# A dilated convolution with gate and projection: thirteen against sixteen six-row groups, and every instruction's place written out

## The chip, the core and the metric

One core of a Trainium2 chip. TensorE does the matrix products into PSUM, VectorE and ScalarE read PSUM and SBUF, GpSimd reads and writes SBUF only, SyncE (SP) issues loads and stores, and 16 DMA engines move the data. The metric is the device time of one execution in microseconds (us): the median of several runs, lower is better.

## What is computed

```python
B, T, D, K = (2, 16000, 256, 3)            # x [B,T,D], w [K,D,2D], w_o [D,D], all bf16
def reference(x, w, w_o):
    dil = 2; pad = (K - 1) * dil
    xp = jnp.pad(x, ((0, 0), (pad, 0), (0, 0)))
    h = jnp.einsum('btc,cd->btd', xp[:, pad:pad + T, :], w[0])
    for i in range(1, K):
        off = pad - i * dil
        h = h + jnp.einsum('btc,cd->btd', xp[:, off:off + T, :], w[i])
    f = h[..., :D]; g = h[..., D:]
    z = jnp.tanh(f) * _sigmoid(g)
    return z @ w_o
```

So h[t] = x[t] w[0] + x[t-2] w[1] + x[t-4] w[2], then a gate, then a projection.

## The kernel before

**Groups.** Time steps are cut into groups. A group has R columns (256 as a rule) and J rows a column: J consecutive time steps. It is computed in four blocks, one for each 128 of the 512 channels of h (two for tanh, two for sigmoid). A block's *product* is two matmuls of 128x128 weights with 2R columns each. There are three kinds of group:

- P, the first 160 columns of the first sequence (J=4): the taps are multiplied directly (`direct`), while weights and inputs are still on their way.
- B (J=4): a fast form of the convolution with four products a block in place of six: m and p with the weights (w0+w2 -+ w1)/2, d0 with w2, d3 with w0. The inputs m, p, d0, d3 are sums or differences of the transposed x (the tile `xt`).
- A (J=6): five products a block for six rows: "first" (u1, with combined weights `wa_sb`), "mid" (rm), "last" (rp), "zero" (r0), "inf" (ri). The inputs u0, u1, u2, e, f are sums of `xt`; u3, uh, ud are u1 times 1/3, -1/2, 2; and rm = e+u3, rp = f+u1, r0 = u0+uh, ri = u2+ud are made on top of e, f, u0, u2.

Sequence one has 6 A, sequence two 7 A, the rest is B: ten with R=256, one with 160, one with 128.

**A block's steps**, as letters of the plan. TensorE: F (first), M (mid, A only), L (last), Z (zero), I (inf); each adds to the PSUM bank b, except I, which adds to the bank a. ScalarE: c copies bank b after F to SBUF (`ss`). VectorE: h makes hh = 1.5 ss - b after M (A only); a makes the bank a = 3 ss + b (A) or -2 ss + b (B) after L, and I is added on top; y makes yy = 2 hh + b (A only). ScalarE then applies tanh or sigmoid to b after Z (letter b), to yy (letter y) and to a after I (letter a). VectorE's g multiplies the tanh and sigmoid parts (`zz`, `zo`). TensorE's P projects a piece of 256 rows with four matmuls of 256 columns, into `o_ps`; e (ScalarE) or v (VectorE) evicts it to `osb`, and SP stores a finished `osb`.

**Who makes the inputs.** VectorE makes u0, u1, u2, e, f, u3, uh, ud, and m, p, d0, d3 of some B groups; GpSimd makes the other B inputs and ri, in quarters of 256 columns. rm, rp, r0 are accumulating DMAs issued from GpSimd's queue (`BY_DMA`). The helper `hold` makes each of GpSimd's sums wait for a VectorE instruction: the one noted last (`made_v[-1]`) or, with n primes on the token, n further back, so that it runs beside a VectorE instruction that reads PSUM.

**The order.** `seq` is the order of the blocks: four B groups, then A and B blocks mixed evenly, then the last B group. `PLAN` has one line for each place k of `seq`; its four columns are the orders of TensorE, ScalarE, VectorE and GpSimd in that place, where block k has its F, block k-1 its L and a, and so on. Loads (transposing DMAs on SP) are issued up to `LOAD = 15` blocks before they are wanted; there are four `xt` buffers for each J. Each engine and each queue runs its own instructions in the order in which they are issued.

Of the kernel before, what the change touches and what calls it, by code (L numbers as in the profile page):

```python
# [11 lines left out]

PLAN = """
 |  | m.0 d3.0 p.0 d0.0 G | 
F D D | c w |  | 
F L D | c d | a d3.1 G | wa.4 wa.3
F L Z I P P | c b e | a | wa.6
Z L F I | a b c | m.1 d0.1 p.1 a | wa.12'
F L Z I | a c b | m.2 g a | wa.5
L P F Z I | a e c b | d3.2 a | wa.2'  # L20
Z L F I | a b c | d0.2 u0.0 g a | wa.7
F L Z I | a c b | f.0 u1.0 a | wa.1
L F Z I | a c b | p.2 a u2.0 g | wa.14'
L Z F I P | a b e c | e.0 d3.3 a | wa.0
F P P Z L I | a c e e b | p.3 ud.0 g a | wa.11
L F I Z P P | a c b | u1.1 m.3 m.4 a | rp.0 ri.0'
F L Z P I P | a e e e b c | u3.0 e.1 uh.0 a d0.3 f.2 g | wa.10
F I Z L P | a c e b | u1.2 a | rm.0 ri.0'
L F Z I | a e c b | a g | r0.0
L Z I F P | a b c | u3.1 p.4 a | wa.8  # L30
Z L F P I | a b c e e | u0.1 uh.2 f.1 a d0.4 g | ri.0'
F I L P Z M P | c e a b | d3.4 u2.1 ud.1 a h | rp.1 rm.1 wa.15' wa.13' wa.9'
F Z L M I | a c e e b | g uh.1 a y h | d3.5' d3.5' ri.0'
P P Z F L I | y a b c | u3.2 e.2 a y | r0.1 ri.1 m.5
F L I Z M | a c y b | a u0.2 h | d0.5 d0.5
Z F L I M | a b c e | g a y h | r0.2 d0.5 ri.1
F P Z I L | a e c b y | g u2.2 a y | rm.2 ri.1 m.5' d0.5
F L P I Z M | a e c y b | a e.3 h | p.5
Z F I L M | a c b | g a y h | p.5 p.5 ri.1
P P F Z L I | a e e y c b | u0.3 a y | m.5 m.5'  # L40
L F I Z M | a c y b | ud.2 a u1.3 h | ri.2 ri.2'
Z P P F L I P M | a b e c e e | g u3.3 a y h | rp.2 p.5' p.6' d0.6'
F Z I L P | a e b c y | f.3 g a y | ri.2 d3.5
F L I Z M | a c y b | a u2.3 h | d3.5
Z F I L M P P | a c b e | g a y h | rp.3 rm.3 d0.6 ri.2
F Z I L P | a e e y b c | uh.3 e.4 ud.3 a y | d3.6 p.6 ri.3''
F L I Z M | a c y b | a u1.4 h | ri.3
Z F I L M P P P | a c b e | g a y h | m.6 d3.6
F Z P L I | a e y c b e e e | g u0.4 u3.4 f.4 a y | r0.3 ri.3 m.6''
F L P I Z M | a c y b | a ud.4 h | d0.6 d3.6 m.6  # L50
Z I F L | a b c | g a y | ri.3 m.6
F L P I Z M P | c a y b | u2.4 a h | ri.4' d3.6
F Z L I P M | a e e c b | e.5 uh.4 y a h | rp.4 p.6
F Z P L I | a y c b e e | g f.5 a y | rm.4 p.6' d0.6'
F P L Z M I | a c y b | g a h | r0.4 p.7 p.7 ri.4 d3.7 d3.7 m.7
F Z L P M I | a c e b e | u1.5 a y h | ri.4
I Z P L F P P | a e e b c y | u0.5 a y | ri.4
F L Z I M | a c b y | ud.5 u1.6 u2.5 a h u3.5 g | rp.5 ri.5''
F P Z L I P M | a c e e b | a y h | rm.5 d0.7 p.7
F Z I L P | a e y b c e | g uh.5 a y | m.7' ri.5  # L60
F L I Z P M | a c y b | g ud.6 a h | r0.5 ri.5' m.7'
F P Z L M I | a c b e e | e.6 uh.6 y a h | d3.7 d0.7
F P Z L I P | y e a b c | f.6 a y | m.7' ri.5
F L Z M I P | a c y b e | u0.6 g h u3.6 a | rp.6 p.7' d0.7' d0.7
F L P M Z I | a c e e e b | y a h | rm.6
Z I L F P | a y b c | u2.6 u1.7 a y g | m.8' m.8'
F P P L Z M I | a c e y b e e | g u3.7 a h | r0.6 ri.6' d3.7'
F Z L P I M | a c b | e.7 ud.7 a y h | p.8' ri.6' ri.6
F Z I L P P | a y b c | u0.7 u2.7 a y | p.8' ri.6'
F L P M Z I | a e c y e e b | uh.7 f.7 a h g | d0.8' ri.7'  # L70
Z I F L | a b c | u1.8 a y | rm.7 rp.7 m.8'
F P P L Z M I | a c e y b e | g a e.8 h | d3.8 ri.7
F Z I L M P | a c b e | g a y ud.8 h | p.8 d3.8 ri.7
F P Z I L P | a e c y b e | u3.8 f.8 a y | r0.7 d3.8' d0.8
L F I Z M P | a e c b y | a u0.8 h | d0.8 m.8
F Z P L P M I P | a c e e e b | e.9 g a y h | p.8 ri.7
Z F L I | a b c y | u1.9 g a y | rp.8 d3.8
F L I Z M P P | a c e b y | u2.8 ud.9 a h | rm.8 d0.8 d3.9'
Z F L P M P I P | a e c e e b | uh.8 g a y h | ri.8 ri.8
Z L F I | y a b e c | u3.9 u2.9 a y | r0.8 ri.8  # L80
F I Z L M P P | a c y b | f.9 u0.9 a h | ri.9' ri.8'
F L Z I M | a e e c b | g y a h | ri.9
F Z I L | y a b c e | f.10 g a y | rp.9 d0.9
F P P L Z M I | c a b y | u0.10 a h | rm.9 d0.9'
F Z I L P P M | a e c e b | e.10 g uh.9 y a h | r0.9 d3.9
F P Z L P I | a e e y b c e | m.9 u1.10 a y | ri.9' ri.9
F L I Z M P | c a e b y | p.9 a h | d0.9' d3.9' d3.9'
Z P F L I M | a b c e e | ud.10 g a y h | d0.9
F I Z P L P | a y b c | u2.10 g a y | rp.10 ri.10 d3.10 d0.10
F L I Z M | a c e y b | a u1.11 h |   # L90
Z P F L P I | a b c e | u3.10 g y uh.10 a | rm.10 ri.10'
F L P Z I M | a e c b e y | e.11 a u2.11 h | ri.10'
F I Z L P P M | c a e b | ud.11 f.11 a y u3.11 h | r0.10 ri.10'
F I Z L | a e c y b e | g uh.11 a y | d3.10 d0.10'
L P F P Z M I | a c b y | g a h | rm.11 d0.10 d3.10
F Z L I M P | a c e b | u1.12 a y h | ri.11' ri.11'
F Z I L | a e c b y | p.10 m.10 y a | rp.11 ri.11
L P F P Z M I | a c e b y e | a u3.12 u0.11 h f.12 g | d3.10
Z F P L I P M P | a c b e | a y h | r0.11 ri.11 d0.10
I F Z L P | a e y e b e c | g e.12 ud.12 y a | rm.12  # L100
F P P M Z L P I | c e a b y e | p.11 u2.12 uh.12 a h g | d3.11' ri.12'
F I L P Z M P | a c e b | y a h | d0.11 d3.11
F Z L P I | y e a b c e e | u0.12 m.11 a y | rp.12 r0.12 ri.12''
F P Z L M I | c a b y | a h g | 
F Z L P I M P | a c b e e e | a y h | d0.11 ri.12
F Z L P I | a c b e y | g a y | d3.11 ri.12
L F I Z M P | a c y b e e | a g h | 
Z F L P I P M | b c a | y a h | 
F P Z L I | a e e y b c e | y a | d0.11
F P L Z M I | c a b y | a h g | d0.11  # L110
F P L Z I P | a e c b e | a y | d3.11
F I Z L | a c y b | g a | 
L P I F Z P | a e b c e | a g | 
Z I F L P P | a c b E | a v | 
L Z I P p | a b | a g v | 
Z I P p P | a e b | v | 
H H | a e E | g v | 
R R |  |  | 
 | e | v | 
# [4 lines left out]
def kernel(  # L124
# [7 lines left out]

    nc = tc.nc
# [15 lines left out]
    LOAD = 15  # L151
# [4 lines left out]
    LEAD, TRAIL = 4, 0  # L156
    N_A = (6, 7)
    groups, of_kind = [], {"P": [], "A": [], "B": []}

    def group(kind, b, t, R):  # L160
        of_kind[kind].append(len(groups))
        groups.append(dict(kind=kind, b=b, t0=t, R=R, J=ROWS[kind]))
        return t + ROWS[kind] * R

    for b in range(B):
        t = 0
        if b == 0:
            t = group("P", b, 0, 160)
        rows = (T - t - 6 * RG * N_A[b]) // 4
        n_a, n_b = N_A[b], rows // RG - (0 < rows % RG < P)  # L170
        for n in range(max(n_a, n_b)):
            if n < n_b:
                t = group("B", b, t, RG)
            if n < n_a:
                t = group("A", b, t, RG)
        rows = (T - t) // 4
        while rows:
            t = group("B", b, t, 160 if rows % P else P)
            rows = (T - t) // 4
    As, Bs = of_kind["A"], of_kind["B"]  # L180
    mixed = [[(g, oi) for g in gs for oi in range(4)] for gs in (As, Bs[LEAD:-1 - TRAIL])]
    seq = [(g, oi) for g in Bs[:LEAD] for oi in range(4)]
    took = [0, 0]
    while took != [len(m) for m in mixed]:
        nxt = 0 if took[0] * len(mixed[1]) < took[1] * len(mixed[0]) else 1
        seq.append(mixed[nxt][took[nxt]])
        took[nxt] += 1
    seq += [(g, oi) for g in Bs[-1 - TRAIL:] for oi in range(4)]
    slot_of = {blk: n for n, blk in enumerate(seq)}
    N = len(seq)  # L190
    assert N == 4 * (len(groups) - 1) == len(slot_of)
    begin = {g: slot_of[g, 0] for g in As + Bs}
    end = {g: slot_of[g, 3] for g in As + Bs}
# [323 lines left out]
    def out_evict(g, rb0, jp, on_v=False):  # L517
# [205 lines left out]
```

## Time and profile before

| | |
|---|---|
| time, median of 3 runs | 263.8 us (262.93 to 263.85) |
| the profiled execution: its span, first to last instruction | 261.4 us |
| what lies between that span and the median | 2.4 us |
| mean granted TensorE clock | 0.999 |
| busy: TensorE, ScalarE, VectorE, GpSimd | 256.5, 243.7, 240.5, 136.2 us |
| accumulating DMAs, loads, stores of whole tiles | 39, 25, 49 |
| DMA packets' share of 16 engines: SP's queue (loads, stores), GpSimd's queue | 54.6%, 23.2% |

The profiler records one execution, and of that one the span is known. Durations are those of single instructions; an engine starts the next instruction before the last one's record ends, so busy time of groups adds up to more than the engine's. PE in the lines is TensorE, DVE is VectorE, ACT ScalarE, POOL GpSimd, SP SyncE.

### The profile page before, as it was taken

How to read it: one execution, taken by the hardware profiler on the slowest of the kernel's cores; microseconds unless marked ns; L12 is line 12 of the kernel's file. 1: busy time of each engine (PE TensorE's matmuls, PEld its weight loads, DVE VectorE, ACT ScalarE, POOL GpSimd, SP SyncE). 2: the span in 40 equal slices, each digit the busy share in tenths (PEclk: the TensorE clock that was granted, in tenths of full speed). 3: DMA queues.
4: the chain of work that ended last, by engine and by line, in shares of the span. 5: the costliest groups of instructions: out<-in, count | busy, mean ns of one | idle time of the engine just before them, and what ended most of it. 6: DMA issues, size and time to landing. Idle time of an engine off the chain costs nothing.

```text
span 261.4 us, 4534 instructions
## 1 busy us (share of the span) xinstructions
PE 256.5 (98%) x1484; PEld 144.2 (55%) x1484; DVE 240.5 (92%) x401; ACT 243.7 (93%) x492; POOL 136.2 (52%) x204
## 2 busy tenths in 40 slices
PE   8999999999999999999999999999999999999993
PEld 5654565545545555555555555555555555665682
DVE  2899999999999999999999999999999999977773
ACT  4989998999999999999999999999999999999993
POOL 1033355687765577956757685643746453431100
PEclk9999999999999999999999999999999999999999
DMA  6999979999969667969895799959825574462115
GB/s 185 215 168 212 262 177 174 227 211 179 212 152 232 139 147 143 228 147 230 197 197 135 175 214 190 239 160 201 237 41 127 149 152 116 129 160 109 76 61 210
DMA packets 81663, 45.20 MB, mean 173 GB/s; under 512 B 68936, under 2 KB 70216, under 8 KB 81640
## 3 DMA queue, kind: packets, MB, share of 16 engines
q1 hardware_dynamic: 75112, 33.74, 54.6%
q0 software_dynamic: 5616, 10.23, 23.2%
q10 hardware_dynamic: 912, 0.95, 1.1%
q8 instruction: 11, 0.18, 0.3%
q14 instruction: 12, 0.10, 0.1%
HBM read 1.25 MB, written 16.38 MB: 67 GB/s over the span
## 4 chain that ended last, share of the span: by engine, by line
PE 97%; DMA 1%; DVE 0%; issue 0%
PE b L401 57%; PE o_ps L512 21%; PE a L401 16%; PE b L421 1%; PE a L421 1%; DMA xn<-in_x_dram 1%; PE tp L308 0%; DVE osb L521 0%; PE fill L248 0%
## 5 line engine op out<-in xcount | busy, mean ns | idle before, releaser
L435 DVE SCALAR_TENSOR_TENSOR a<-ss,b 128x512 f32<-128x512 f32 (+2 forms) x100 | 67.1, 672 | 7.9 <-ACT sg L475 3.1
L537 ACT CAST osb<-o_ps 128x512 bf16<-128x512 f32 x119 | 69.8, 622 | 0.8 <-PE o_ps L512 0.7
L512 PE MATMUL o_ps<-wo_sb,zz 128*128 128x256 bf16 x496 | 70.5, 273 | 0.0
L432 ACT COPY ss<-b 128x512 f32<-128x512 f32 (+2 forms) x100 | 59.6, 597 | 4.6 <-PE b L401 3.5
L512 PEld LDWEIGHTS <-zz 128*128 128x128 bf16 x496 | 48.4, 98 | 25.2 <-DVE zz L494 0.2
L401 PEld LDWEIGHTS <-w_sb 128*128 128x128 bf16 x400 | 39.0, 98 | 36.8 <-issue 0.2
L382 POOL TENSOR_TENSOR u<-u,ud 128x256 bf16<-128x256 bf16 x52 | 39.8, 772 | 24.9 <-DVE zz L494 9.1
L382 POOL TENSOR_TENSOR d<-xt 128x256 bf16<-128x256 bf16 (+2 forms) x56 | 33.4, 606 | 32.7 <-DVE zz L494 13.0
L494 DVE TENSOR_TENSOR zz<-th,sg 128x1536 bf16<-128x1536 bf16 (+2 forms) x52 | 40.9, 788 | 0.5 <-ACT sg L475 0.2
L435 DVE SCALAR_TENSOR_TENSOR yy<-hh,b 128x512 f32<-128x512 f32 x52 | 35.4, 680 | 1.9 <-PE b L401 1.8
L435 DVE SCALAR_TENSOR_TENSOR hh<-ss,b 128x512 f32<-128x512 f32 x52 | 35.4, 681 | 1.2 <-PE o_ps L512 0.5
L475 ACT ACTIVATE sg<-b 128x512 bf16<-128x512 f32 (+2 forms) x50 | 30.5, 610 | 2.1 <-PE b L401 1.4
L475 ACT ACTIVATE th<-b 128x512 bf16<-128x512 f32 (+2 forms) x50 | 30.5, 610 | 1.9 <-PE b L401 1.6
L475 ACT ACTIVATE sg<-a 128x512 bf16<-128x512 f32 (+2 forms) x50 | 31.0, 619 | 0.0
L401 PE MATMUL b<-f,wp_sb 128*128 128x512 bf16 x104 | 30.9, 379 | 0.0
L401 PE MATMUL b<-u,w_sb 128*128 128x512 bf16 x104 | 30.9, 379 | 0.0
L401 PE MATMUL a<-u,w_sb 128*128 128x512 bf16 x104 | 30.9, 379 | 0.0
L401 PE MATMUL b<-u,wa_sb 128*128 128x512 bf16 x104 | 30.9, 379 | 0.0
L401 PE MATMUL b<-e,wm_sb 128*128 128x512 bf16 x104 | 30.9, 378 | 0.0
L475 ACT ACTIVATE th<-a 128x512 bf16<-128x512 f32 (+2 forms) x50 | 30.5, 614 | 0.3 <-PE a L401 0.2
L401 PEld LDWEIGHTS <-wp_sb 128*128 128x128 bf16 x200 | 19.5, 98 | 20.1 <-issue 0.7
L401 PEld LDWEIGHTS <-wm_sb 128*128 128x128 bf16 x200 | 19.5, 98 | 17.0 <-issue 0.4
(59 smaller groups left out, 342.7 us busy)
## 6 DMA issues: line engine op xcount, KB each, us to landing
out_dram<-osb SPq DMA_DIRECT2D x26, 384.0 KB, 2.6
out_dram<-osb SPq DMA_DIRECT2D x23, 256.0 KB, 3.0
f<-u POOLq DMA_DIRECT2D x13, 256.0 KB, 3.5
e<-u POOLq DMA_DIRECT2D x13, 256.0 KB, 4.4
u<-uh POOLq DMA_DIRECT2D x13, 256.0 KB, 5.3
w_sb<-in_w_dram ACTq DMA_DIRECT2D x3, 256.0 KB, 4.1
xt<-in_x_dram SPq DMA_TRANSPOSE x25, 7.2
xn<-in_x_dram SPq DMA_DIRECT2D x1, 160.0 KB, 3.2
```

Source lines behind the costliest of these rows:

```text
L382: ins = eng.tensor_tensor(out=o, in0=a, in1=b, op=op)
L401: nc.tensor.matmul(G[bank, oi][:, :2 * R], lhsT=wmat[:, ct, osl], rhs=G[mv][:, :, ct, :R], start=which == "first" and ct == 0, stop=ct == ...
L421: nc.tensor.matmul(G[bank, oi][:, :4 * r].rearrange("p (j r) -> p j r", j=4), lhsT=w_taps[tap][:, ct, osl], rhs=xt[:, j0:j0 + 4, ct, c0 + ...
L432: nc.scalar.copy(out=G["ss", oi][:, :n], in_=G["b", oi][:, :n])
L435: return note(nc.vector.scalar_tensor_tensor(out=out, in0=in0, scalar=scalar, in1=in1, op0=ALU.mult, op1=op))
L475: nc.scalar.activation(out=G[name, dt][:, j:j + 2, :R], in_=G[bank, oi][:, :2 * R].rearrange("p (q r) -> p q r", q=2), func=(ACT.Tanh, ACT ...
L494: note(nc.vector.tensor_tensor(out=G["z"][:, dt, :, :n], in0=G["th", dt][:, :, :n], in1=G["sg", dt][:, :, :n], op=ALU.mult))
L512: nc.tensor.matmul(o_ps[:, q, :], lhsT=z, rhs=wo_sb[:, dt, :], start=dt == 0 and (q == 0 or len(dts) == NT), stop=dt == NT - 1, skip_group ...
L537: copy(out=osb[:, 2 * jp:2 * jp + 2, :], in_=o_ps[:])
```

## The change

1. **Sixteen A groups.** `GROUPS` lists the groups by hand: P160, 8 A, 3 B in sequence one; 8 A, 2 B, then B of 128, 160 and 128 in sequence two. B groups are thus five with R=256, one with 160, two with 128. `ORDER` lists the blocks: three B groups (12 blocks), then A blocks with now and then a block of a B group of the other sequence, then the last B128.
2. **Second ScalarE copies.** 22 of the 64 A blocks no longer have h on VectorE: ScalarE copies bank b after M (`k`), and yy is then made as -2 hh + a, from the bank a (before I is added) and not from b. The other 42 keep h.
3. **One list for all.** `PLAN` is a single list of 1,782 instructions; each engine and queue takes its own in the list's order. It names each eviction (102 on ScalarE, 24 on VectorE), each store (`s`), and each load after the first four (`x`).
4. **Inputs.** rm, rp, r0 and ri are accumulating DMAs in 15 of 16 groups each (60 in all; before 39); the other four are made by GpSimd (three) and VectorE (one). GpSimd makes 132 quarters of A inputs (e, f, u0, u1, u2 of some groups, and the three) and 56 of B inputs. VectorE makes 51 full sums and 48 scalings for A, and 18 sums for B. A token like `u1.3q24` is a quarter held behind the VectorE instruction noted 24 further back than the last.
5. **Buffers.** The pools of the inputs, `th`/`sg` and `osb` become one pool with the same numbers of slots, picked by the order of the groups. The scratch for the combined weights moves from the `hh`/`yy` buffers to the `zz` buffers.

The diff, cut to its core (the list is shown by its start and end):

```diff
+GROUPS = (
+    "P160 A A A A A A A A B B B",
+    "A A A A A A A A B B B128 B160 B128",
+)
+ORDER = """
+9 9 9 9 10 10 10 10 11 11 11 11 1 20 1 1 1 2 20 2 2 2 3 20 3 3 3 4 20 4 4 4 5 21 5 5 5 6 21 6 6 6 7 21 7 7 7 8 21 8
+8 8 12 23 12 12 12 13 23 13 13 13 14 23 14 14 14 15 23 15 15 15 16 22 16 16 16 17 22 17 17 17 18 22 18 18 18 19 22
+19 19 19 24 24 24 24
+"""
 PLAN = """
...
-F L Z I | a c b | m.2 g a | wa.5
...
+p.0 m.0 d3.0 d0.0 F m.1 F c D d0.1 c D L w p.1 D L A wa.0q6 d F wa.5q3 A Z wa.4q3 c x I G b Z u0.0 L b G F a f.0 I c
+F d3.1 a d0.2q11 P A c L g e0 P x Z A e1 I b d3.2 Z a P u1.0 F b u2.0 s0 L d0.2q1 c x I A e2 F wa.8q4 a L m.2 d0.2q2
...
+I v116 c L P a A e117 L P b A s44 e118 I g Z s43 a v119 P b I v120 P a Z P s45 b P e121 g H v122 e123 H R R s46 e124
+v125 s47
 """
-    LOAD = 15
...
+    SLOTS = {"m": 2, "p": 2, "d0": 3, "d3": 3, "u0": 3, "u1": 3, "u2": 3, "e": 3, "f": 3, "u3": 2, "uh": 2, "ud": 2, "hh": 3, "th": 2, "osb": 3, "odd": 3}
...
-    wu_sb = [[ss_pool.tile([P, D2], f32, name=f"wu{tap}", tag=tag) for tag in ("hh", "yy")] for tap in range(K)]
+    wu_ct = [z_pool.tile([P, K, D2], f32, name="wu", tag="zz6") for _ in range(CT)]
+    wu_sb = [[wu_ct[ct][:, tap, :] for ct in range(CT)] for tap in range(K)]
...
-    BY_DMA = ("rm", "rp", "r0")
...
-        if name in BY_DMA:
+        if eng is None:
             return nc.gpsimd.dma_start(out=G[name][:, :, :, :R], in_=b, accum_op=op)
...
-    def halfway(blk):
+    def second(blk, on_act):
...
-        G["hh", oi] = ss_pool.tile([P, 2 * RG], f32, name="hh")
+        G["hh", oi] = slot("hh", a_seq.index(blk), [P, 2 * RG], f32)
+        if on_act:
+            G["k", oi] = True
+            nc.scalar.copy(out=G["hh", oi][:, :n], in_=G["b", oi][:, :n])
+            return
         stt(G["hh", oi][:, :n], G["ss", oi][:, :n], 1.5, G["b", oi][:, :n], ALU.subtract)
...
-            stt(G["y", oi][:, :n], G["hh", oi][:, :n], 2.0, b)
+            if ("k", oi) in G:
+                stt(G["y", oi][:, :n], G["hh", oi][:, :n], -2.0, G["a", oi][:, :n])
+            else:
+                stt(G["y", oi][:, :n], G["hh", oi][:, :n], 2.0, b)
...
+    def on_gpsimd(token):
+        token, _, back = token.partition("q")
+        behind = made_v[-1 - int(back)]
...
+        pre(g, name, nc.gpsimd, slice(had, had + 1), behind=behind)
...
+    for token in PLAN.split():
+        what = token[0]
+        if "." in token:
+            if "q" in token:
+                on_gpsimd(token)
+            elif token[-1] == "d":
+                pre(*group_of(token[:-1]), None)
             else:
...
+                note(pre(*group_of(token), nc.vector))
+        elif what in "FMLZI":
+            product(next(kinds[what]), {"F": "first", "M": "mid", "L": "last", "Z": "zero", "I": "inf"}[what])
...
+        elif what in "hk":
+            second(a_seq[int(token[1:])], what == "k")
...
+        elif what in "ev":
+            out_evict(*pieces[int(token[1:])], on_v=what == "v")
+        elif what == "s":
+            store(*stores[int(token[1:])])
+        elif what == "x":
+            load(next(to_load))
```

More of the change, by code (lines that the diff above doesn't have):

```diff
@@ L465, in activate @@
         if (name, dt) not in G:
-            G[name, dt] = act_pool.tile([P, J, RG], bf16, name=name, tag=f"{name}{J}")
+            same = [at for at in blocks if groups[at]["J"] == J]
+            G[name, dt] = slot(f"{name}{J}", NT * same.index(g) + dt, [P, J, RG], kind="th")
         if G["kind"] == "P":
```

388 lines of the change are left out of this document (128 added, 260 removed).

## The prediction

> **What bounds the kernel now.** I read the page first (busy time, clock, chain), then the busy time by stretches, then the matrix engine's timeline.
>
> ```profile
> span 261.4 us, 4534 instructions
> ...
> PE 256.5 (98%) x1484; PEld 144.2 (55%) x1484; DVE 240.5 (92%) x401; ACT 243.7 (93%) x492; POOL 136.2 (52%) x204
> ...
> PE 97%; DMA 1%; DVE 0%; issue 0%
> ```
> ```profile
> 0.00:20.00 20.00, 19.16 (x122) 11.23 (x123) 14.00 (x25) 14.98 (x31) 3.35 (x13) 1.00 0.96 190
> 20.00:220.00 200.00, 200.00 (x1111) 108.27 (x1109) 195.58 (x323) 191.62 (x379) 124.48 (x176) 1.00 0.86 182
> 220.00:256.00 36.00, 36.00 (x246) 23.77 (x244) 29.52 (x53) 35.73 (x82) 8.38 (x15) 1.00 0.36 112
> 256.00:261.40 5.40, 1.30 (x12) 0.92 (x10) 1.41 (x3) 1.35 (x3) 0.00 (x0) 0.96 0.52 199
> ```
> Each row of the second fence gives a stretch, its length, then busy time and instructions of PE, PEld, DVE, ACT and POOL, the clock, the DMA share (1.00 is all 16 engines) and GB/s. TensorE is busy 200.00 of the 200 us from 20 to 220, 36.00 of the next 36, and it is 97% of the chain. So every matmul taken out shortens the kernel, if nothing else takes its place. The same rows warn: from 20 to 220 VectorE is busy 195.58 (98%) and ScalarE 191.62 (96%). VectorE's slack is at the end (29.52 of 36), ScalarE's at the start.
>
> A busy matmul is not a matmul's price, since they overlap, so prices here are distances from start to start.
>
> ```profile
> 47.82 0.59 PE L401 MATMUL b<-u,wa_sb 128*128 128x512 bf16 x2
> 48.25 0.59 PE L401 MATMUL b<-d,w_sb 128*128 128x512 bf16 x2
> ```
> ```profile
> 253.00 0.38 PE L401 MATMUL b<-p,wp_sb 128*128 128x256 bf16 x2
> 253.21 0.38 PE L401 MATMUL b<-d,w_sb 128*128 128x256 bf16 x2
> ```
> A pair (one product) with 512 columns costs 0.43 us, one with 256 columns 0.21.
>
> **TensorE.** Groups before: 13 of kind A (6 rows a column, 4 blocks of 5 products), and of kind B (4 blocks of 4 products) 10 with R=256, one 160, one 128. After: 16 A, and B 5 with 256, one 160, two 128. Products with 512 columns fall from 13x20+10x16=420 to 16x20+5x16=400, those with 256 columns rise from 16 to 32; the output projection and the direct group stay. 20x0.43=8.6 less, 16x0.21=3.4 more: **5.2 us less**, all on the chain, as TensorE is never idle after the start.
>
> **VectorE and ScalarE.** The new list names each instruction, so they can be counted. Prices, start to start:
>
> ```profile
> 102.40 0.68 DVE L435 SCALAR_TENSOR_TENSOR yy<-hh,b 128x512 f32<-128x512 f32 x1
> 103.00 0.95 DVE L494 TENSOR_TENSOR zz<-th,sg 128x1536 bf16<-128x1536 bf16 x1
> 103.87 0.69 DVE L435 SCALAR_TENSOR_TENSOR a<-ss,b 128x512 f32<-128x512 f32 x1
> ```
> ```profile
> 105.06 0.98 DVE L382 TENSOR_TENSOR u<-xt 128x1024 bf16<-128x1024 bf16 x1
> 106.06 0.70 DVE L435 SCALAR_TENSOR_TENSOR a<-ss,b 128x512 f32<-128x512 f32 x1
> ```
> ```profile
> 30.18 0.42 DVE L380 TENSOR_SCALAR ud<-u 128x1024 bf16<-128x1024 bf16 x1
> 30.51 0.68 DVE L494 TENSOR_TENSOR zz<-th,sg 128x1024 bf16<-128x1024 bf16 x1
> ```
> ```profile
> 103.27 0.69 ACT L475 ACTIVATE th<-yy 128x512 bf16<-128x512 f32 x1
> 103.81 0.64 ACT L475 ACTIVATE th<-b 128x512 bf16<-128x512 f32 x1
> ```
> ```profile
> 105.18 0.59 ACT L432 COPY ss<-b 128x512 f32<-128x512 f32 x1
> 105.66 0.59 ACT L537 CAST osb<-o_ps 128x512 bf16<-128x512 f32 x1
> ```
> From each start to the next: 0.60 for a combine, 0.87 for a wide gate, 0.33 for a scaling (a sum or a middle gate, 0.68 long as a combine, is taken at 0.60); on ScalarE 0.48 for a copy, taken for evictions and activations too, and 0.54 for a yy. Narrow forms I estimate at half.
> - VectorE: combines a 100 to 96 (eight fewer wide, four more narrow), -3.6; hh 52 to 42, -6.0; yy 52 to 64, +7.2; full sums of A 65 to 51, -8.4; sums of B 26 to 18, -4.8; scalings 39 to 48, +3.0; gates 26 to 32 wide, 20 to 10 middle, two more narrow, -0.2; evictions 5 to 24, at a combine's price, +11.4. Sum -1.4: about 239 us.
> - ScalarE: first copies 100 to 96 (-2.9), the new second copies 0 to 22 (+10.6), activations of b and a 200 to 192, eight more of them narrow (-5.8), of yy 52 to 64 (+6.5), evictions 119 to 100 (-9.1). Sum -0.7: about 243.
>
> Neither grows, but both must fit into a span 5 us shorter: 239 and 243 of 256, or 93% and 95%. VectorE lacks 6.0 us of the first 20 and 4.0 of the last 5.4, so it has 246 us of room, and 7 to spare. I cost these edits at nothing: 98% did not stop TensorE in 20 to 220, and the new list spreads the work (20 of the 24 evictions on VectorE stand after 130 us of matmuls). With a second copy, yy is made from the a bank, so TensorE's product I waits for yy as well as for a. In the list 0.86 us of matmuls or more stand between such a yy and its I, over the 0.68 the yy takes.
>
> **GpSimd.** Quarter sums rise from 140 to 188; they now include e, f, u0, u1 and u2 of A, which VectorE made. DMA issues rise from 39 to 60.
>
> ```profile
> L382 POOL TENSOR_TENSOR u<-u,ud x52: 658/667/1125, 33.1 to 236.4; 128x256 bf16<-128x256 bf16 x52
> L382 DVE TENSOR_TENSOR u<-xt x39: 673/685/1215, 21.7 to 227.8; 128x1024 bf16<-128x1024 bf16 x39
> ...
> L377 POOL DMA_DIRECT2D e<-u x13: 857/869/1177, 36.1 to 221.7; - x13
> ```
> At most 48x0.67+21x0.87=50 more: 186 of 256, 73%. It hides under TensorE: what GpSimd makes is mostly wanted 2 to 15 us of matmuls later.
>
> **The DMAs.** Sums added by DMA go from three an A group to four, 39 to 60 (four stay on engines); loads and stores keep their bytes.
>
> ```profile
> q1 hardware_dynamic: 75112, 33.74, 54.6%
> q0 software_dynamic: 5616, 10.23, 23.2%
> ```
> ```profile
> q1 hardware_dynamic: 12304, 4.25, 85.3%
> q0 software_dynamic: 866, 1.58, 33.4%
> ...
> e<-u POOLq DMA_DIRECT2D x2, 256.0 KB, 8.4
> xt<-in_x_dram SPq DMA_TRANSPOSE x5, 10.2
> ```
> Over the span (first fence) q1 takes 142.7 us of 16 engines, q0 60.6. With 60/39 of the latter, 93.3, both make 236 of 256, 92%. The second fence is the DMA view of 40 to 70 us, the densest stretch: 119% of packet time, and the e sums take 8.4 us to land, while TensorE loses nothing (it lies in the row 20 to 220).
> Between a DMA sum's place in the list and the first matmul that reads it stand 5.6 to 22 us of matmuls, about 11 in the middle. If all landed as in 40 to 70 (8.4 us), eight first users would come up short, by 2.3, 0.2, 1.9, 0.6, 2.8, 0.2, 1.9 and 1.3 us: 11 us. If they land as the median of the whole trace, 4.4, none does.
>
> ```profile
> DMA to landing us min/median/max: 3.3/4.4/10.9
> ```
> I take **0.8 us**, near the low end: in the list the short distances stand away from the loads, and the 4.4 is the nearer row for those.
> Loads stand 12 to 31 us ahead of their first use for A, 6 to 12 for the later B, against the 10.2 they take in that stretch. A late B load holds GpSimd, the first to read it in most cases, by at most 10.2-5.6=4.6 us, which GpSimd's idle quarter takes.
> Stores, now placed one by one, and loads share SP's queue, and a store waits there for its last eviction, with the loads behind it. The lead of the loads covers this; if it did not, the sums and their first products would be late by the excess.
>
> **The start.** VectorE's list now begins with p, m, d3, d0 of the first group, then three sums of the second group, ahead of the first combine.
>
> ```profile
> 7.38 10.94 SPq L234 DMA_TRANSPOSE xt<-in_x_dram  x3
> ```
> ```profile
> 11.13 0.69 DVE L382 TENSOR_TENSOR d<-xt 128x1024 bf16<-128x1024 bf16 x1
> ```
> ```profile
> 13.40 0.70 DVE L435 SCALAR_TENSOR_TENSOR a<-ss,b 128x512 f32<-128x512 f32 x1 [1.10 <-PE b L401]
> 14.00 0.69 DVE L382 TENSOR_TENSOR d<-xt 128x1024 bf16<-128x1024 bf16 x1
> ```
> Before, the combine ran at 13.40 and the second group was first read at 14.00, without a wait. The fourth of the first group's sums started at 11.13 and takes 0.6, so the second group is now read at 11.7. Its load (the first of the three issued at 7.38) lands between 11.7 and 14.0, so the combine runs between 11.7+1.8=13.5 and 15.8, and behind it TensorE waits 0.1 to 2.4 us. I take the middle, **1.2 us**.
>
> **Sum.** Span 261.4-5.2+0.8+1.2=258.2. The median of the runs shown is 263.8, 2.4 above the span; kept, that is **260.6 us**, 1.2% faster. With both costs hidden: 258.6.
>
> **Rivals.** A measurement of this kernel can tell about 0.5%, 1.3 us, from no change.
> - *GpSimd meets VectorE (slower).* Before, each quarter sum was held until a VectorE instruction just ahead had ended, and ran beside a combine. Now 156 of the 188 are held behind an instruction more than ten back, which is as good as free. A VectorE sum or gate that meets one can lose: the u sum at 105.06 held the engine 1.00 us and not 0.60. The list has 119 such instructions (69 sums, 50 gates); the spare 7 us are gone after 18 hits of 0.40. If a third are hit, that is 16 us, 9 beyond the spare: 258.6+9=267.6. For it: GpSimd's sums would fill half of the time. Against it: the u<-xt row's median is 685 and its minimum 673, so few were hit, though GpSimd was 62% busy from 20 to 220; and in the list most quarters stand beside combines. Chance 0.17. The Trainium skill (SBUF — State Buffer, Who interferes with whom) states that a VectorE instruction with two SBUF inputs contends with a GpSimd one that reads SBUF, and that the second to issue "fully blocks" until the first has finished; at 0.67 us a quarter that would be an estimated 0.33 a meeting and, with half of the 119 meeting one, some 20 us and 271. The u<-xt row shows it only in its tail (1215).
> - *DMA sums late (no change).* If the density of 40 to 70 us became the rule, the 11 us of shortfalls would count, but a TensorE that waits once gives the later ones time; I take half: 258.6+5.5=264.1. For it: 92% of packet time throughout. Against it: 119% went unpunished. Chance 0.13.
> - *ScalarE becomes the bound (no change).* The change would then not do what it says: work moves to ScalarE and TensorE waits for it. If ScalarE can be kept only as full as from 20 to 220 (96%), its 243 us need 253, with the 9 it lacks at the start and the end 262: 264.5. For it: it loses nothing by the change, and the span shrinks. Against it: from 220 to 256 it was busy 35.73 of 36 and TensorE never waited. Chance 0.06.
>
> **How the numbers follow.** The forecast has 0.64: faster by over 0.5% (below 262.5) gets that; same 0.17 (DMA sums and ScalarE, but for 0.02); slower 0.19 (GpSimd, and those 0.02). The forecast's own range is 258.4 to 262.4. For 8 in 10 it must take in the DMA rival and the lighter half of the GpSimd rival: 258.4 to 266.4.
>
> **What would show it.** Right: 800 matmuls of 512 columns in the products, TensorE's busy time near 251, the chain still above 95% PE, a VectorE wait for a load at 12 to 14 us and a TensorE gap soon after. VectorE near 239, GpSimd near 186, DMA sums landing at 4 to 7 us. Wrong: TensorE idle for several us in the middle, and behind it DMA sums (second rival), or VectorE's u and zz rows far above 690 and 950 ns (first rival).

## The result, and the profile after

The changed kernel takes 277.3 us (median of three runs, 276.61 to 278.64) against 263.8 before: 1.053 times as long [1.049, 1.058]. The prediction said 260.6 us, faster, and at most 266.4; the kernel is 5% slower. The profiled execution took 276.61 us, with a span of 274.8. (Some executions were disturbed, over 1.5% longer than the best of their kernel or at a lower clock; they are left out of all ratios and of the times of e6 and e8 below, and of e1 and e6 no profile is used.)

The page of the changed kernel, with busy times and the chain:

```profile
span 274.8 us, 4673 instructions
...
PE 256.2 (93%) x1476; PEld 144.2 (52%) x1476; DVE 257.9 (94%) x403; ACT 244.0 (89%) x495; POOL 184.6 (67%) x273
...
PE 68%; DVE 17%; issue 6%; DMA 4%; SPq 2%; ACT 1%; DVEq 0%
```

Before, TensorE was 97% of the chain; now it is 68%, and VectorE holds 17%. ScalarE's 244.0 and GpSimd's 184.6 us are what was forecast (243 and 186). VectorE's 257.9 are 19 more than the forecast's 239, with the instructions that were counted. The same by stretches (columns as in the prediction):

```profile
20.00:60.00 40.00, 38.66 (x204) 19.54 (x202) 39.80 (x66) 36.80 (x74) 27.86 (x40) 1.00 1.09 211
60.00:100.00 40.00, 37.55 (x211) 20.44 (x209) 39.86 (x60) 36.27 (x73) 32.89 (x50) 1.00 1.09 202
100.00:140.00 40.00, 39.13 (x219) 21.33 (x218) 39.39 (x63) 39.12 (x79) 34.55 (x48) 1.00 0.94 205
140.00:180.00 40.00, 39.67 (x229) 22.30 (x229) 39.68 (x67) 38.70 (x80) 35.92 (x52) 1.00 1.09 212
180.00:220.00 40.00, 34.96 (x206) 19.82 (x204) 39.90 (x59) 34.37 (x71) 33.57 (x51) 1.00 0.81 177
```

From 20 to 220 us TensorE was busy 200.00 of 200 before; now it has 190.0. The engine that is full is VectorE: 198.6 of 200. The waits name it too (total, times, longest):

```profile
PE a L339 <- DVE a L373: 5.6, 4, 2.5
PE b L339 <- DVE a L373: 5.2, 5, 2.3
...
DVE m L320 <- DMA xt<-in_x_dram: 0.9, 1, 0.9
```

TensorE waits for VectorE's combine `a`. It was not the combine that had grown. One of the longest waits, in VectorE's timeline, then GpSimd's, then TensorE's:

```profile
93.49 0.68 DVE L320 TENSOR_TENSOR e<-xt 128x1024 bf16<-128x1024 bf16 x1
94.10 3.98 DVE L440 TENSOR_TENSOR zz<-th,sg 128x1536 bf16<-128x1536 bf16 x1
98.01 0.68 DVE L373 SCALAR_TENSOR_TENSOR a<-ss,b 128x512 f32<-128x512 f32 x1
```
```profile
94.47 0.97 POOL L320 TENSOR_TENSOR u<-xt 128x256 bf16<-128x256 bf16 x1
95.11 0.96 POOL L320 TENSOR_TENSOR f<-xt 128x256 bf16<-128x256 bf16 x1
95.73 1.52 POOL L320 TENSOR_TENSOR u<-xt 128x256 bf16<-128x256 bf16 x2
```
```profile
98.74 0.59 PE L339 MATMUL b<-u,w_sb 128*128 128x512 bf16 x2 [2.25 <-DVE a L373]
```

A gate that took 0.95 us in the trace of before takes 3.98. In that time GpSimd runs four quarter sums with no pause between them (the gate starts at 94.10, they run from 94.47 to 97.25), and the gate ends after the last of them. The combine behind it starts at 98.01, and TensorE has stood still for 2.25 us. There are few such instructions, and a median does not see them:

```profile
L320 DVE TENSOR_TENSOR u<-xt x32: 678/684/2223, 17.7 to 225.4; 128x1024 bf16<-128x1024 bf16 x32
L318 DVE TENSOR_SCALAR uh<-u x16: 410/418/2630, 26.6 to 230.3; 128x1024 bf16<-128x1024 bf16 x16
...
L440 DVE TENSOR_TENSOR zz<-th,sg x50: 411/949/3982, 16.3 to 268.8; 128x1536 bf16<-128x1536 bf16 x32, 128x1024 bf16<-128x1024 bf16 x10, 128x512 bf16<-128x512 bf16 x8
```

The medians of `u` and `uh`, 684 and 418 ns, are those of before (685 and 418), and 949 is what a wide gate took then (0.95 us); the maxima, 2223, 2630 and 3982, are several times as long. The scaling `uh` reads only one tensor and is hit as hard.

### The profile page after: what moved, and what is told of

The parts are those of the page before. It is cut to its first block, busy times and chain, and to the rows that moved or that the text cites. A ratio compares the mean times of both kernels' runs of the same rounds, so it can differ in the third digit from the quotient of the medians.

```text
span 274.8 us, 4673 instructions
## 1 busy us (share of the span) xinstructions
PE 256.2 (93%) x1476; PEld 144.2 (52%) x1476; DVE 257.9 (94%) x403; ACT 244.0 (89%) x495; POOL 184.6 (67%) x273
## 3 DMA queue, kind: packets, MB, share of 16 engines
q1 hardware_dynamic: 74648, 33.74, 52.4%
q0 software_dynamic: 8640, 15.73, 33.8%
## 4 chain that ended last, share of the span: by engine, by line
PE 68%; DVE 17%; issue 6%; DMA 4%; SPq 2%; ACT 1%; DVEq 0%
PE b L339 41%; PE o_ps L458 16%; PE a L339 11%; DVE a L373 5%; DMA xt<-in_x_dram 3%; DVE yy L373 3%; SPq L170 2%; DVE uh L318 2%; DVE u L320 1%; DMA w_sb<-in_w_dram 1%; DVE hh L373 1%; DVE zz L440 1%; DVE p L320 1%; DVE osb L467 1%; DVE e L320 0%
## 5 line engine op out<-in xcount | busy, mean ns | idle before, releaser
L373 DVE SCALAR_TENSOR_TENSOR a<-ss,b 128x512 f32<-128x512 f32 (+2 forms) x96 | 62.6, 656 | 2.7 <-PE b L339 1.6
L475 ACT CAST osb<-o_ps 128x512 bf16<-128x512 f32 x100 | 59.2, 614 | 0.7 <-PE o_ps L458 0.5
L320 POOL TENSOR_TENSOR u<-xt 128x256 bf16<-128x256 bf16 x64 | 55.2, 938 | 2.6 <-PE a L339 2.0
L440 DVE TENSOR_TENSOR zz<-th,sg 128x1536 bf16<-128x1536 bf16 (+2 forms) x50 | 49.1, 987 | 0.6 <-ACT sg L421 0.6
L339 PE MATMUL a<-u,w_sb 128*128 128x512 bf16 x128 | 38.1, 379 | 5.8 <-DVE a L373 5.6
L339 PE MATMUL b<-u,w_sb 128*128 128x512 bf16 x128 | 38.2, 383 | 3.6 <-DVE a L373 2.3
L339 PE MATMUL b<-f,wp_sb 128*128 128x512 bf16 x128 | 38.4, 382 | 0.2 <-DVE hh L373 0.2
L339 PE MATMUL b<-e,wm_sb 128*128 128x512 bf16 x128 | 38.0, 380 | 0.0
L320 POOL TENSOR_TENSOR d<-xt 128x128 bf16<-128x128 bf16 (+2 forms) x36 | 28.0, 803 | 12.0 <-DMA xt<-in_x_dram 4.8
L320 POOL TENSOR_TENSOR e<-xt 128x256 bf16<-128x256 bf16 x32 | 26.7, 862 | 13.3 <-PE b L339 5.8
L421 ACT ACTIVATE sg<-b 128x512 bf16<-128x512 f32 (+2 forms) x48 | 28.4, 591 | 3.7 <-PE b L339 3.4
L373 DVE SCALAR_TENSOR_TENSOR yy<-hh,b 128x512 f32<-128x512 f32 x42 | 28.5, 678 | 1.4 <-PE b L339 1.4
L373 DVE SCALAR_TENSOR_TENSOR hh<-ss,b 128x512 f32<-128x512 f32 x42 | 28.4, 680 | 0.5 <-PE b L339 0.2
```

Source lines behind the costliest of these rows:

```text
L320: ins = eng.tensor_tensor(out=o, in0=a, in1=b, op=op)
L339: nc.tensor.matmul(G[bank, oi][:, :2 * R], lhsT=wmat[:, ct, osl], rhs=G[mv][:, :, ct, :R], start=which == "first" and ct == 0, stop=ct == ...
L373: return note(nc.vector.scalar_tensor_tensor(out=out, in0=in0, scalar=scalar, in1=in1, op0=ALU.mult, op1=op))
L421: nc.scalar.activation(out=G[name, dt][:, j:j + 2, :R], in_=G[bank, oi][:, :2 * R].rearrange("p (q r) -> p q r", q=2), func=(ACT.Tanh, ACT ...
L440: note(nc.vector.tensor_tensor(out=G["z"][:, dt, :, :n], in0=G["th", dt][:, :, :n], in1=G["sg", dt][:, :, :n], op=ALU.mult))
L475: copy(out=G["osb", at][:, 2 * jp:2 * jp + 2, :], in_=o_ps[:])
```

## The experiments

Two theories, and one beside them. *Reads*: GpSimd's sums, let loose by the far holds, take VectorE's SBUF reads away, most where several run back to back. *Load*: the new list asks VectorE or TensorE for something that does not fit, whoever reads SBUF. *DMA*: sums added by DMA come late.

### Near holds: e1, e2

The list, the groups and all instructions stay; only the hold of GpSimd's sums changes.

```diff
-        behind = made_v[-1 - int(back)]
+        behind = made_v[-1]                       # e1
+        behind = made_v[-1 - min(int(back), 1)]   # e2
```

> The changed kernel, in which every GpSimd sum is held behind the VectorE instruction that stands last before it in the list (and not one up to hundreds further back); nothing else differs. Port theory: in the changed kernel VectorE spends some 20 us (257.9 busy against 238 by instruction prices) waiting, inside instructions that read two SBUF operands or scale, for GpSimd sums that run back to back. Held one by one they must run beside combines again: VectorE's busy time falls to 240 to 246 us, the 4 us gate at 94 us is gone, and the time falls from 277.3 to 260 to 268, less what late GpSimd sums cost. Load theory (VectorE has too much to do in a shorter span, the holds don't matter): VectorE stays at 255 to 258, the time at 275 to 280.

> The changed kernel with every GpSimd sum held behind the VectorE instruction one before the last in the list (or the last, where the list says so). Port theory: GpSimd can run one VectorE instruction early, so it meets more sums and gates than when held behind the last: VectorE busy 243 to 250, time 262 to 271, between that kernel and the changed one. Load theory: 275 to 280 as the changed kernel.

Measured: e1 273.9 us, 1.036 times before [1.029, 1.042]. e2 264.7 us, 1.005 [1.002, 1.009]. One edit to the holds gives back 12.6 of the 13.5 us. In e2's page VectorE lost 10.4 us of its busy time with the same 403 instructions:

```profile
span 263.2 us, 4685 instructions
...
PE 253.6 (96%) x1476; PEld 143.7 (55%) x1476; DVE 247.5 (94%) x403; ACT 243.1 (92%) x495; POOL 182.8 (69%) x273
```

So the hold is the cause, not the load of the list. But e1 missed its range (260 to 268): the latest hold should have been the better of the two and is the worse, which is taken up below.

### GpSimd writes but does not read: e3

Each quarter sum becomes two fills of the same quarter of the same tile, about as long together; the 60 DMA issues and the far holds stay. Left out are the quarter sums, and with them GpSimd's waits for their inputs.

```diff
-        if op is None:
+        if eng is nc.gpsimd and name not in ON_TOP:
+            eng.memset(o, 0.0)
+            ins = eng.memset(o, 0.0)
+        elif op is None:
```

> The changed kernel in which each GpSimd quarter sum is left out and two fills of the same quarter with zeros stand in its place: GpSimd writes as before but reads nothing, its 60 DMA issues stay, and the holds stay as far back as they are. Port theory (reads through a port shared with VectorE): VectorE's busy time falls to 238 to 241 and the time to 258 to 263. DMA theory (what slows VectorE is the issuing of 60 accumulating DMAs, or their traffic): VectorE stays above 250 and the time above 270. Load theory: the same, above 270.

Measured: 260.6 us, 0.989 [0.984, 0.994], and the prediction's own span (258.2) to within 0.2 us:

```profile
span 258.4 us, 4855 instructions
...
PE 251.8 (97%) x1476; PEld 143.7 (56%) x1476; DVE 240.2 (93%) x403; ACT 242.4 (94%) x495; POOL 166.1 (64%) x449
...
PE 89%; DVE 4%; DMA 3%; SPq 1%; ACT 1%; issue 1%; ACTq 0%
```

GpSimd is busy 166 us, its 60 DMA issues are all there, and VectorE is not disturbed (240.2): neither the DMA sums nor the load of the list slow it. Where the 17.7 us to 257.9 lie shows in the groups of VectorE, the changed kernel first and e3 second:

```profile
L440 DVE TENSOR_TENSOR zz<-th,sg 128x1536 bf16<-128x1536 bf16 (+2 forms) x50 | 49.1, 987 | 0.6 <-ACT sg L421 0.6
...
L318 DVE TENSOR_SCALAR uh<-u 128x1024 bf16<-128x1024 bf16 x16 | 9.1, 575 | 0.0
L320 DVE TENSOR_TENSOR p<-xt 128x1024 bf16<-128x1024 bf16 (+1 forms) x6 | 8.8, 1460 | 0.0
```
```profile
L443 DVE TENSOR_TENSOR zz<-th,sg 128x1536 bf16<-128x1536 bf16 (+2 forms) x50 | 40.6, 816 | 0.6 <-ACT sg L424 0.6
...
L323 DVE TENSOR_TENSOR p<-xt 128x1024 bf16<-128x1024 bf16 (+1 forms) x6 | 4.4, 731 | 0.0
L321 DVE TENSOR_SCALAR uh<-u 128x1024 bf16<-128x1024 bf16 x16 | 7.1, 448 | 0.0
```

Gates 8.5 us more, six sums `p` 4.4, the sums `u` 2.5 (24.3 and 21.8), the scalings `uh` 2.0. The combines `a`, `hh` and `yy`, which read PSUM, do not differ (62.6 and 62.9, 28.4 and 28.5, 28.5 and 28.5 us).

Set against the same 403 instructions of e3, one by one, 17 are longer by over 0.25 us in the changed kernel, together by 17.6 us. Six of them, by 1.5 to 3.3 us each, make 13.2 of it, and beside each of the six run three to six GpSimd sums.

On TensorE, the distances from each matmul's start to the next, as far as they exceed 0.216 us for 512 columns (0.109 for 256, others in proportion), add up to 21.9 us in the changed kernel, 10.3 in e2 and 5.5 in e3. The differences to e3, 16.4 and 4.8, are the differences of the spans (274.8, 263.2, 258.4): the loss lies between the matmuls and not at the ends. What they wait for is in the waits: those of TensorE that end with a VectorE instruction add up to 13.1 us in the changed kernel and 1.1 in e3.

### The kernel before with far holds: e4

If far holds are the cause, they must hurt the old list too, with its 140 quarter sums.

```diff
-            behind = made_v[-1 - token.count("'")]
+            behind = made_v[max(0, len(made_v) - 31)]
```

> The kernel before, with its GpSimd sums held behind the VectorE instruction 30 back and so as good as free; the work and the order are those of before. Port theory: back-to-back GpSimd sums now meet VectorE's sums and gates: VectorE's busy time rises from 240.5 by 5 to 12 us and the time from 263.8 to 266 to 274. Load theory (it is the sixteen groups and the shorter span that overload VectorE): the time stays within 1 us of 263.8.

Measured: 315.1 us, 1.194 [1.189, 1.200]. The hold alone is worth 51 us in the kernel before. The direction is the one expected, the size is not (266 to 274): in the kernel before, the near holds keep off far more than the 4% that was thought. VectorE's busy time rises from 240.5 to 284.7:

```profile
PE 271.4 (87%) x1484; PEld 146.2 (47%) x1484; DVE 284.7 (91%) x401; ACT 247.4 (79%) x492; POOL 140.4 (45%) x204
```
```profile
176.75 7.82 DVE L494 TENSOR_TENSOR zz<-th,sg 128x1536 bf16<-128x1536 bf16 x1
```

One gate took 7.82 us. GpSimd's busy time went up by only 4 us (136.2 to 140.4): not how much GpSimd runs decides, but when. Part of the 51 us is TensorE's clock: its mean in e4 is 0.956, against 0.999 before.

### The engines alone: e7

No convolution: VectorE's sums, scalings and combines of the kernel's sizes, beside GpSimd's quarter sums that run free or held, and beside fills (shortened: the stretches' count is written as 16, and `held` puts a sum behind each VectorE sum).

```python
stretch([v_sum] * 16, [])                              # undisturbed
stretch([v_sum] * 16, [g_sum] * 24)                    # free sums beside
stretch([v_scale] * 16, [g_sum] * 16)
stretch([v_combine] * 16, [g_sum] * 16)
stretch([v_sum, v_combine] * 16, [g_sum] * 32)         # free
stretch([v_sum, v_combine] * 16, [g_sum] * 16, held)   # each beside a combine
stretch([v_sum] * 16, [g_fill] * 40)                   # writes only
```

> Not the convolution: seven stretches of VectorE and GpSimd instructions of this kernel's shapes on constant data, nothing else running. 1: 16 VectorE sums alone (0.60 us each). 2: the same beside free GpSimd quarter sums. 3: 16 scalings beside them. 4: 16 combines reading PSUM beside them. 5: 16 times a sum and a combine in turn beside them. 6: the same, one GpSimd sum held behind each VectorE sum, so that it runs beside the combine. 7: 16 sums beside free GpSimd fills that read nothing. Port theory: stretches 2, 3 and 5 stretch to well over their 10, 5.5 and 19 us, with single VectorE instructions of 1.2 us and more; 4, 6 and 7 stay within 10% of 10, 19 and 10 us. If the slowing in the kernel comes from DMA issues or traffic, none stretches.

VectorE's timeline (start, us, instructions; equal ones that follow each other are one row), and two rows of GpSimd's:

```profile
35.48 12.97 DVE L66 TENSOR_SCALAR vo<-va 128x1024 bf16<-128x1024 bf16 x16 [5.55 <-POOL go L74]
48.59 9.66 DVE L70 SCALAR_TENSOR_TENSOR vq<-vf,pb 128x512 f32<-128x512 f32 x16
58.70 20.46 DVE L62 TENSOR_TENSOR vo<-va,vb 128x1024 bf16<-128x1024 bf16 x1 [0.44 <-POOL go L74]
...
119.73 9.72 DVE L62 TENSOR_TENSOR vo<-va,vb 128x1024 bf16<-128x1024 bf16 x16 [0.24 <-POOL go L74]
```
```profile
48.60 30.01 POOL L74 TENSOR_TENSOR go<-ga,gb 128x256 bf16<-128x256 bf16 x48 [0.43 <-DVE vo L66]
98.63 0.67 POOL L74 TENSOR_TENSOR go<-ga,gb 128x256 bf16<-128x256 bf16 x1 [20.02 <-DVE vo L62]
```
```profile
99.06 0.78 DVE L62 TENSOR_TENSOR vo<-va,vb 128x1024 bf16<-128x1024 bf16 x1
99.77 0.68 DVE L70 SCALAR_TENSOR_TENSOR vq<-vf,pb 128x512 f32<-128x512 f32 x1
100.36 0.84 DVE L62 TENSOR_TENSOR vo<-va,vb 128x1024 bf16<-128x1024 bf16 x1
```

- One VectorE sum took **20.46 us**: it began while GpSimd's sums ran back to back (48.60 to 78.61), and ended half a microsecond behind the last of them. It was starved for the whole run, not for one GpSimd instruction.
- Sixteen scalings took 12.97 us, 0.81 each from start to start, where the prediction's rows give 0.33. So an instruction with a single SBUF operand can be hit.
- Sixteen combines, which read one operand from SBUF and one from PSUM, took 9.66 us beside GpSimd's sums, 0.60 each, as if alone. So did sixteen sums beside fills (9.72): writes by GpSimd cost VectorE nothing.
- A GpSimd sum held so that it starts with a combine costs the sum behind it 0.10 to 0.16 us (0.78 to 0.84 against 0.68). The held stretch took 21.6 us in all, 13% above the expected 19 and not within 10%; and in the second and third stretch no instruction reached the expected 1.2 us (1.15 and 0.89 at most).

The Trainium skill (SBUF — State Buffer, Who interferes with whom) states that a VectorE instruction with at most one SBUF input does not contend, except for forms such as `tensor_scalar` in a two-port mode, and that a GpSimd instruction that only writes does not disturb one with two inputs. Combines, scalings and fills here agree; in which mode the scalings ran no run shows. The same page (Summary: rules for kernel authors) has the second to issue wait until the first finishes; the 20.46 us do not fit one first instruction, since 32 passed ahead of one.

### Which near hold: e5, e6, e8 to e12

Can a hold keep the new list's gain? All are the changed kernel with another choice of `behind` (lines that only keep count are left out).

```diff
-        behind = made_v[-1 - int(back)]
# e5: the sum starts with a PSUM-reading instruction, if the last one noted is one
+        n = len(made_v) - 1
+        if reads_psum(noted[n]):
+            n -= 1
+        behind = made_v[n]
# e6: as e5, and no two sums behind the same instruction
+        n = max(n, min(used[0] + 1, len(made_v) - 1))
# e8: as e1, made_v[-1]
# e9, e10: at most two, at most four back
+        behind = made_v[-1 - min(int(back), 2)]
# e11: from the listed hold on, the first free place ahead of a PSUM-reading instruction
+        last = len(made_v) - 1
+        free = range(max(last - int(back), used[0] + 1), last)
+        used[0] = max(used[0], next((n for n in free if reads_psum(noted[n + 1])), last))
# e12: from the listed hold on, two VectorE instructions apart
+        used[0] = max(used[0], min(last, max(last - int(back), used[0] + 2)))
```

> The changed kernel, each GpSimd sum held so that it starts together with a VectorE instruction that reads PSUM: if the VectorE instruction last listed before it is a combine, an hh, a yy or an eviction, behind the one before that; else behind the last. Port theory: fewer sums start into VectorE sums and gates than with every sum held one back (264.7 us, VectorE 247.5): VectorE 243 to 247, time 261 to 264.5. If it is only lateness of GpSimd that matters (held behind the last one gave 273.9): 265 to 272.

> As the kernel held beside PSUM readers, and besides no two GpSimd sums are held behind the same VectorE instruction unless it is the last listed, so that they do not run back to back. Port theory in its stronger form (it is sums running back to back that starve VectorE): VectorE 240 to 244, time 259.5 to 263, if GpSimd keeps up. Lateness: GpSimd falls behind and the time is 265 to 275.

> The kernel with every GpSimd sum held behind the last listed VectorE instruction, once more, for its profile (the first one's time was 273.9). Port theory with lateness: VectorE's instructions are no longer stretched much (busy under 247), and the time goes to TensorE and VectorE waiting for sums that GpSimd starts too late. If holding does not keep VectorE free, its busy time is above 250 again.

> Each GpSimd sum held behind the VectorE instruction noted at most two further back than the last (the version with at most one further back gave 264.7, the last itself 271 to 274, the listed holds 277.3). Starvation theory (a GpSimd sum costs VectorE little when it is held close, much when several run back to back): the sums lose part of their spacing, since a sum held two back may start early and the next behind it follows at once; VectorE's excess between the 11.5 us of one back and the 19.8 of the listed holds, 266 to 271. Lateness theory (what is left at one back are inputs that come late): two back is earlier, so faster, below 264.

> As with at most two, but up to four further back. Starvation theory: nearer to the listed holds, 269 to 276, VectorE's busy time 251 to 257. Lateness theory: no slower than with two back, 263 to 265.

> Each GpSimd sum held behind the first VectorE instruction at or after its listed hold that has a PSUM-reading instruction as its successor and behind which no other sum is held yet (the last one noted, if there is none). The sums keep most of the lead that the list gives them, but each comes beside a PSUM-reading instruction and no two are released together. Starvation theory: VectorE's excess falls to or below that of one back (11.5 us), with the sums less late: 260 to 265 us; VectorE busy below 248. If sums wait in GpSimd's queue and pile up anyway, they run back to back behind a late one, and it is 268 to 274.

> As e11_spread_beside, but each sum is held two VectorE instructions behind the one before it, whatever that instruction reads (not before its listed hold, and never behind more than the last one noted). Starvation theory: spacing alone keeps sums from running back to back; 262 to 267, VectorE busy 243 to 250. If it is the partner and not the spacing that counts, half of the sums meet a sum or gate at 0.2 to 0.4 us each, 20 to 38 us over e3's VectorE time, and it is above 270.

All of them in the order of VectorE's busy time in their pages:

| kernel | hold | VectorE busy, us | time, us | ratio to before |
|---|---|---|---|---|
| e3 | far, GpSimd only writes | 240.2 | 260.6 | 0.989 [0.984, 0.994] |
| before | near, 140 quarter sums | 240.5 | 263.8 | 1 |
| e2 | at most one back | 247.5 | 264.7 | 1.005 [1.002, 1.009] |
| e5 | beside a PSUM read | 249.1 | 265.6 | 1.010 [1.007, 1.014] |
| e11 | spread, beside PSUM reads | 251.3 | 269.2 | 1.025 [1.017, 1.033] |
| e8 (e1) | the last | 251.7 | 269.1 (273.9) | 1.021 (1.036 [1.029, 1.042]) |
| e12 | spread, two apart | 254.0 | 271.0 | 1.030 [1.025, 1.035] |
| e9 | at most two back | 254.1 | 272.1 | 1.035 [1.032, 1.037] |
| e10 | at most four back | 255.1 | 274.2 | 1.041 [1.037, 1.045] |
| the changed kernel | as listed, mostly over ten back | 257.9 | 277.3 | 1.053 [1.049, 1.058] |

e6, without a profile to use, took 268.0 and 271.7 us, 1.024 [1.018, 1.031]. (e8's ratio is that of the medians, 269.1 and 263.6, without an interval; e8 and e1 are the same kernel, so its executions spread over 2%.) From one back to two, to four, to the listed holds the time rises step by step. That falsifies the thought that an earlier sum is at least not slower, which e9 and e10 also put to the test. Over the rows the time rises with VectorE's busy time, whatever the rule of the hold. The groups are worth 1.1% where nothing meets VectorE (e3), and no hold that was tried keeps that: no version beats the kernel before.

Most of the new expectations failed. e2, e3 and e10 came within their ranges, and e9 missed its own by 1 us. e5 (261 to 264.5 expected, VectorE 243 to 247) is no better than e2, and e6 (259.5 to 263) is worse: aiming each sum at a PSUM read, or one sum at one instruction, does not bring the gain back. e11 (260 to 265) came out at 269.2, in the range for sums that pile up anyway (268 to 274). e12 (262 to 267) lies just in its "above 270", where the partner and not the spacing counts, but VectorE lost 13.8 us against e3 and not the 20 to 38 named for that. e11 and e12 did not get the spacing that they asked for, since a hold is only the earliest start: 82% and 79% of their quarter sums still begin without a pause (0.1 us or less) behind another GpSimd instruction (56% before, 87% in e2, 91% in the changed kernel). In e11 two sums released one by one still ran in one piece behind two DMA issues, beside a gate:

```profile
136.53 1.34 POOL L320 TENSOR_TENSOR u<-xt 128x256 bf16<-128x256 bf16 x1
137.17 2.05 POOL L320 TENSOR_TENSOR f<-xt 128x256 bf16<-128x256 bf16 x1
```
```profile
136.26 2.45 DVE L440 TENSOR_TENSOR zz<-th,sg 128x1536 bf16<-128x1536 bf16 x1
```

What the holds change shows when VectorE's instructions are set against the same ones in e3, by the number of GpSimd sums that run beside them (us lost; in brackets how many lose over 0.05 us; the instructions beside no sum, 0.6 to 0.9 us shorter in all, count in the last column alone):

| kernel | one sum | two sums | three or more | in all |
|---|---|---|---|---|
| e2, at most one back | 1.9 (16) | 4.4 (12) | 2.5 (2) | 8.2 |
| e8, the last | 7.2 (29) | 4.6 (14) | 1.4 (1) | 12.3 |
| e9, at most two back | 2.7 (14) | 9.9 (18) | 3.0 (2) | 14.8 |
| e10, at most four back | 2.4 (15) | 2.5 (14) | 11.8 (7) | 15.8 |
| the changed kernel | 2.3 (15) | 2.2 (12) | 14.6 (8) | 18.5 |

From one back on, the further back the hold, the more sums one VectorE instruction meets; a long one also meets more because it is long, so the table alone does not tell cause from effect. It does tell why the last is worse than one back: not by sums that pile up (85% begin without a pause in e8, 87% in e2), but by more instructions that meet a single one, as in e11 and e12 too (26 and 29 of them, 6.7 and 7.5 us). Why those are more stays open. No list was tried with other places for the GpSimd sums and DMA issues.

## Why the prediction was wrong, by its steps

**TensorE, 5.2 us less: right.** With VectorE undisturbed (e3), span and TensorE's busy time (258.4, 251.8) came out at 258.2 and "near 251". That the span fits to 0.2 us is partly luck: of the 2.0 us that the sum adds for DMA sums and the start, e3 shows no wait for a DMA sum and 1.1 us of waits for combines, of which the longest ends at 20.2, and 0.6 us that the sum lacks lie at the end (5.0 us from the last matmul's start, 4.4 before).

**VectorE "about 239", ScalarE "about 243": right as sums of undisturbed durations** (240.2 and 242.4 in e3). The second copies cost what was counted, and in e3 TensorE never waited for a yy. ScalarE as the bound (the third rival) is refuted: in e3, where ScalarE is busy 94% of the span, it is 1% of the chain.

**The DMAs: right.** The two queues took 52.4% and 33.8% of 274.8 us, 237 us; the prediction said 236.

```profile
u<-ud POOLq DMA_DIRECT2D x15, 256.0 KB, 5.0
u<-uh POOLq DMA_DIRECT2D x15, 256.0 KB, 4.8
e<-u POOLq DMA_DIRECT2D x15, 256.0 KB, 4.6
f<-u POOLq DMA_DIRECT2D x15, 256.0 KB, 5.7
```

They land within the forecast 4 to 7 us. The second rival is refuted: no wait of TensorE over 0.04 us ends with a DMA sum, neither in the changed kernel nor in e3 (e2 has one, 0.83 us for `f`). The 0.8 us taken for it were too much.

**The start: right in kind.** VectorE waits 0.9 us for the load (row above), and TensorE 0.92 us behind it, until 15.7; 1.2 was taken.

**"I cost these edits at nothing", and GpSimd "hides under TensorE": this is the step that failed.** GpSimd's own time did hide (184.6 us of the 186 forecast). What did not hide is what its reads do to VectorE: not nothing, but 17.7 us of busy time (257.9 against 240.2 in e3) and with it 16.4 us of span. The first rival named the mechanism and the place, and got a chance of 0.17. Three things in that rival were wrong:

- *The evidence against it.* The median of 685 ns was read as "few were hit, though GpSimd was 62% busy". But the near holds had made it so; e4 takes them away and loses 51 us. That trace showed the protection at work, not that there was nothing to protect from.
- *The price of a hit.* 0.40 us came from one `u` sum at 105.06, beside the end of one quarter and the start of the next. In the changed kernel 17 VectorE instructions lose 17.6 us, and six of them 13.2, each beside a run of quarters. Few hits, up to 3.3 us each, and not a third of 119 at 0.40. The 48 scalings, left out of the 119, were hit too. That the sum of the rival, 16 us, lies near the measured 17.7 all the same is luck: too many hits, too cheap.
- *The spare.* The rival let 7 us of it vanish in VectorE's idle time and reached 267.6. But hits fall in the middle, and there little was idle: from 20 to 220, 4.7 us in e3 and 1.4 in the changed kernel, so 3.3 took up part of the 17.7. The other 14.4 went into the span, which is 16.4 longer; of the 2.0 that remain, TensorE's slower clock explains 1.65 (below).

The rule of the Trainium skill, weighed in the prediction, came to 271, nearer than the forecast, but for a price of 0.33 a meeting that the runs do not show either.

What was to show the error, "u and zz rows far above 690 and 950 ns", held for the longest and the mean (zz 987 against 816 in e3), not for the medians (684 and 949).

## What to carry to other kernels

A cheap-looking hold or wait in a tuned kernel can be what keeps two engines apart: before counting contention as small because a trace shows little of it, ask what in that trace prevents it, and look at the longest instances, not the median. Where an instruction moves to an engine that reads the same memory, its cost is paid by the other engine, and few hits can make the whole cost: in e7 one sum lost 20 us behind 32 free quarters, while 16 quarters held apart cost 2.4 us in all (21.6 us against 32 times 0.60). A hold is only an earliest start, so it does not by itself keep such instructions apart in a busy queue. Spare time counts only where the hits fall.

## What the runs showed of the hardware that had not been expected

**Starving.** A VectorE sum or gate can stand behind a whole run of GpSimd sums: 20.46 us behind 32 of them in e7, 7.82 in e4, 3.98 in the changed kernel. To begin first did not protect the last of these: the gate at 94.10 began 0.37 us before the first of the four sums that it outlasted. In e7 it did not always do so: in the second stretch, sixteen VectorE sums beside free GpSimd sums took 16.7 us, 1.04 each (from GpSimd's first sum at 13.26 to VectorE's last at 29.94). There the engines took turns, one sum of each every 1.07 us, and GpSimd's sums took 1.11 us too and not 0.67. What decides between sharing and starving was not tested.

**The clock after a wait.** TensorE's 2.00 us wait at 233.57 in the changed kernel was followed by slow matmuls, in its timeline and in a window (granted clock 0.73, the third figure from the end):

```profile
233.57 0.59 PE L339 MATMUL a<-u,w_sb 128*128 128x512 bf16 x2 [2.00 <-DVE a L373]
...
234.92 1.91 PE L458 MATMUL o_ps<-wo_sb,zz 128*128 128x256 bf16 x8
236.63 1.06 PE L339 MATMUL b<-u,w_sb 128*128 128x512 bf16 x2
237.48 0.95 PE L339 MATMUL b<-f,wp_sb 128*128 128x512 bf16 x2
238.27 0.38 PE L339 MATMUL b<-m,wm_sb 128*128 128x256 bf16 x2
```
```profile
232.00:238.00 6.00, 4.43 (x18) 2.34 (x18) 5.10 (x8) 3.15 (x7) 3.50 (x6) 0.73 0.41 132
```

Eight matmuls of 256 columns took 1.71 us from start to start (at 0.21 a pair, 0.84), and the two pairs behind them 0.85 and 0.79 where 0.43 is usual: 1.65 us, on top of the wait. After the waits of 2.25 and 2.48 us that end at 98.74 and 218.80 the granted clock was 1.00, and in e10 it was 1.00 after a wait of 2.00 us that ends at 230.99, so the length of the wait alone does not decide it. After e4's wait of 6.78 us the clock was 0.52 for the next 6 us.
